# The scores of batch 1 moved into the transform of batch 0, and x of batch 2 transposed on TensorE

## The chip, the cores and the metric

The kernel runs on one core of a Trainium2 chip, in one launch. The metric is the device time of one execution in microseconds (us); less is better. Everything is written by hand for five engines: PE (TensorE, matrix products and transposes), ACT (ScalarE), DVE (VectorE), POOL (GpSimd) and SP, which issues most of the transfers.

## The reference

Two blocks follow each other. The first is an attention between 512 rows of `x` and 32 rows of `state` for each of 8 batches and 8 heads; the second mixes the 544 rows that come out with a two-dimensional Fourier transform, of which the real part is kept, then normalises each row and runs a two-layer network over it.

```python
def _attn_ref(x, state):                       # x (8, 8, 512, 64), state (8, 8, 32, 64)
    scores = scale * np.matmul(x, state.transpose(0, 1, 3, 2))
    a = softmax over the last axis of scores
    xread = np.matmul(a, state)
    scores2 = scale * np.matmul(state, x.transpose(0, 1, 3, 2))
    a2 = softmax over the last axis of scores2
    sread = np.matmul(a2, x)
    return np.concatenate([xread, sread], axis=2)

def _moe_ref(x, w_ch1, w_ch2):                 # x (8, 544, 512), w (512, 2048) and (2048, 512)
    mixed = np.real(np.fft.fft(np.fft.fft(x, axis=1), axis=2))
    u = x + mixed
    un = (u - mean) / np.sqrt(var + 1e-06)     # over the last axis
    return u + np.maximum(un @ w_ch1, 0.0) @ w_ch2
```

## The kernel before

The work goes batch by batch, and each batch passes five stages.

- **Load and cast.** `load_x(b)` brings x of a batch into the buffer `xs` (two of them, in turn), and `cast_x(b)` writes it as bf16 into `xin` (`xin0` for even batches, `xin1` for odd ones). From batch 1 on, the cast is one instruction on POOL (L117).
- **Attention, first half** (`attend`, its list `first`). The products need x and state with the other axis on the partitions: `turn_state` transposes state on PE into the PSUM tile `sTp`, and a copy (L311) makes `sT` of it. `turn_x(g)`, for g = 0 and 1, makes `xT` of x. For batches 0 and 1 it transposes on PE into the PSUM tile `xTp` (L322), with a copy by DVE for g = 0 and by ACT for g = 1 (L323). For batches from `by_dma` = 2 on, it is four transposing transfers, which SP issues (L316). `scores_t(g)` then forms `eTp` (L331) and its exponential `ET` on ACT (L333); `scores(i)` forms `esp` (L342) and `E` (L347).
- **Attention, second half** (`second`). `xread` and `sread` multiply `ET` and `E` with state and x (PSUM tiles `xrp`, `xfp`, `xlp`, `srp`), DVE divides by the sums, and `fold` adds and subtracts halves of the result on DVE to make `XE`, `XO` and `XN`.
- **Transform** (`transform`). `over_s(j)` is the transform over the rows (`gp`, L455 and L459; its copy `G`, L461 and L463), `over_d(k)` the one over the columns (`yp`, L473). `add(k, r)` makes a tile of `U` on DVE, `centre(k, r)` takes its statistics on DVE and subtracts the mean (`ub`, L490 on ACT), and `turn_u(k, r)` transposes `ub` into `unT`: on PE (`tp`, L501) with a copy by ACT (L502) for batches 0 and 1, by a transposing transfer later.
- **Network.** `layer1(b)` multiplies `unT` with the first weights (`ph`, L587 for batch 0 in quarter steps of 16 products of 128 columns, L577 for the others), and ACT writes `hT` (L589, L579). `layer2(b)` multiplies `hT` with the second weights (`po`, L643), DVE forms the output tile `ot` (L608), and SP stores it.

Both weights (`w` in the profile's rows) come through POOL's queue: the first from L254, the second from L269, which stands behind a small POOL instruction that reads the landed x of batch 2 (L267).

The order is written out by hand. Each engine executes its instructions in the order in which the program names them, and `weave` merges lists of steps: each list is spread evenly over a stretch from 0 to 1, and the steps are named in the order of these places. Every list here is so merged with the layer-1 or layer-2 products of an earlier batch. Three PSUM banks serve `sTp`, `xTp`, `eTp`, `esp`, `srp`, `gp`, `yp` and `tp` in turn (`qt`), three others serve `ph` and `po`, one pair serves `xread`. `warm(n)` puts n products without use on PE; `warmed` puts them behind each step of a list.

The program's middle names first the start of the transform of batch 0, then layer 1 of batch 0 with the rest of that transform (`t0[7:]`), with both halves of batch 1 (`s1` and `reads_next`), with the transform of batch 1 and with the first half of batch 2 (`scores_next`). `cast_x(2)` and the transfers that transpose x of batch 2 (`turned[2]`) stand at one tenth of it:

```python
for step in warmed(t0[:7], 2):
    step()
load_x(3)
scores_next, reads_after = attend(2)
weave((layer1(0), 0, 1), (t0[7:], 0.02, 0.3), (s1, 0.02, 0.32), (reads_next, 0.33, 0.57),
      (transform(1), 0.61, 1.0), ([lambda: (cast_x(2), turned[2]())], 0.1, 0.1), (scores_next, 0.5, 0.95),
      ([lambda: state_ones(2, B)], 0.5, 0.5), ([lambda: load_x(4)], 0.8, 0.8))
```

Of the kernel before, what the change touches and what calls it, by code (L numbers as in the profile page):

```python
# [28 lines left out]
def kernel(  # L29
# [8 lines left out]
    nc = tc.nc  # L38
# [72 lines left out]
    def cast_x(b):  # L111
        xs, t = xs_of[b], xin_bufs[b % 2]
        if b == 0:
            for si in (0, 1, 3, 2):
                nc.scalar.copy(t[:, si, 1:513], xs[:, si, :])
        else:
            nc.gpsimd.tensor_copy(t[:, :, 1:513], xs)  # L117
# [153 lines left out]
    def qt(name, dt=F32):  # L271
        return psQ.tile([128, 512 if dt == F32 else 1024], dt, name=name, tag="q")
# [12 lines left out]
        return mv, rstd  # L285


    by_dma = 2


    turned = {}

    def attend(b):
# [6 lines left out]
        sT = wk.tile([128, 4, 128], BF16, name="sT", tag="sT")  # L300
# [5 lines left out]
        def turn_state():  # L306
            p = qt("sTp", BF16)
            for pr in range(4):
                g, hp = pr // 2, pr % 2
                nc.tensor.transpose(p[:, pr * 128:(pr + 1) * 128], sb[:, g, 4 + 128 * hp:132 + 128 * hp], ident)  # L310
            nc.vector.tensor_copy(sT, p[:, 0:512].rearrange("p (a b) -> p a b", b=128))  # L311

        def turn_x(g):
            if b >= by_dma:
                for si in ((0, 1), (3, 2))[g]:
                    nc.sync.dma_start_transpose(out=xT[:, :, 128 * si:128 * si + 128], in_=xin[:, si, 1:513])  # L316
                return
            p = qt("xTp", BF16)
            for si in (0, 1, 3, 2):
                for k in range(2):  # L320
                    o = k * 512 + si * 128
                    nc.tensor.transpose(p[:, o:o + 128], xin[:, si, 1 + 128 * (2 * g + k):129 + 128 * (2 * g + k)], ident)  # L322
            (nc.vector.tensor_copy if g == 0 else nc.scalar.copy)(  # L323
                xT[:, 2 * g:2 * g + 2, :], p.rearrange("p (a b) -> p a b", b=S))


# [77 lines left out]
        def fold():  # L404
# [5 lines left out]
            nc.vector.tensor_sub(XO[:, 0:2, 1:256], Sm[:, :, 1:256], Sm[:, :, 511:256:-1])  # L410
            nc.vector.tensor_copy(XN[:, 0:2, 0:1], Sm[:, :, 256:257])

        first = ([] if b >= by_dma else [turn_state, lambda: turn_x(0), lambda: turn_x(1)]) + [
            lambda: scores_t(0),
            lambda: scores_t(1),
            lambda: scores(0),
            lambda: scores(1),
        ]
        if b >= by_dma:
            turned[b] = lambda: (turn_x(0), turn_x(1))  # L420
            first.insert(0, turn_state)
        second = [
# [15 lines left out]
    def transform(b):  # L438
        g4, bq = b // 4, b % 4
        XF, XR = XFs[b % 2], XRs[b % 2]  # L440
        XE, XO, XN = XEs[b % 2], XOs[b % 2], XNs[b % 2]
        G = wk.tile([128, 4, NM], BF16, name="G", tag="G")
        cos = [CT[:, 0, :], CT[:, 1, :], CL[:, bq, :]]
        sin = [ST[:, 0, :], ST[:, 1, :], SL[:, bq, :]]
        unT = wk.tile([128, DC, 512], BF16, name="unT", tag="unT", bufs=2)
        un_of[b] = unT
        U, ub, rstds = {}, {}, {}
        order = [(0, 1), (1, 1), (0, 0), (1, 0)] if b == B - 1 else [(0, 1), (0, 0), (1, 1), (1, 0)]

        def over_s(j):  # L450
            p = qt("gp")
            X, tab = (XE, cos) if j < 2 else (XO, sin)
            jj = j % 2
            for c in range(3):
                nc.tensor.matmul(p[:, 0:NM], lhsT=X[:, c, 128 * jj:128 * jj + 128], rhs=tab[c],  # L455
                                 start=(c == 0), stop=(c == 2 and j != 2))
            if j == 2:
                for c in range(3):
                    nc.tensor.matmul(p[:, 0:NM], lhsT=XN[:, c, :], rhs=cos[c], start=False, stop=(c == 2))  # L459
            if b == 0 and j < 2:  # L460
                nc.vector.tensor_copy(G[:, j, :], p[:, 0:NM])  # L461
            else:
                nc.scalar.copy(G[:, j, :], p[:, 0:NM])  # L463
            if j == 3:
                nc.gpsimd.tensor_copy(GLs[g4][:, :, 32 * bq:32 * bq + 32], G[:, :, 256:NM])  # L465

        yp_of = {}

        def over_d(k):
            U[k] = wk.tile([128, 2, 514], F32, name="U", tag="U", bufs=5)  # L470
            yp = yp_of[k] = qt("yp")
            for c in range(4):
                nc.tensor.matmul(yp, lhsT=G[:, c, 128 * k:128 * k + 128], rhs=T2[:, c, :],  # L473
                                 start=(c == 0), stop=(c == 3))

        def add(k, r):
            yp = yp_of[k]
            if r:
                nc.vector.tensor_add(U[k][:, 1, 1:512], yp[:, 1:512], XR[:, k, 1:512])  # L479
                nc.vector.tensor_add(U[k][:, 1, 512:513], yp[:, 0:1], XR[:, k, 512:513])  # L480
            else:
                nc.vector.tensor_add(U[k][:, 0, 0:512], yp, XF[:, k, 0:512])

        def centre(k, r):
            u = U[k][:, r, r:r + 512]
            mv, rstds[k, r] = stats_of(u, "rstd")
            t = ub[k, r] = wk.tile([128, 512], BF16, name="ub", tag="ub", bufs=5)
            ud = u if r == 0 else U[k][:, 1, 512:0:-1]
            if b in flipped:
                nc.scalar.activation(t, ud, AF.Identity, bias=mv[:, 0:1], scale=-1.0)  # L490
            else:
                nc.vector.tensor_scalar(t, in0=ud, scalar1=mv[:, 0:1], scalar2=None, op0=ALU.subtract)

        def turn_u(k, r):
            col = order.index((k, r)) * 128
            if b >= by_dma:
                nc.sync.dma_start_transpose(out=unT[:, :, col:col + 128], in_=ub[k, r])
                return
            tp = qt("tp", BF16)
            for j in range(DC):  # L500
                nc.tensor.transpose(tp[:, 128 * j:128 * j + 128], ub[k, r][:, 128 * j:128 * j + 128], ident)  # L501
            nc.scalar.copy(unT[:, :, col:col + 128], tp[:, 0:512].rearrange("p (a b) -> p a b", b=128))  # L502

        def done():
            tiles = []
            for k, r in order:
                if True:
                    u = U[k][:, r, 0:512] if r == 0 else U[k][:, r, 512:0:-1]
                    f0 = 128 * k + 1
                    dst = out[b, f0:f0 + 128, :] if r == 0 else (b, k)  # L510
                    tiles.append((u, rstds[k, r], dst))
            tiles_of[b] = tiles

        if b == 0:
            return [lambda j=j: over_s(j) for j in range(4)] + [
                lambda: over_d(0),
                lambda: (add(0, 1), centre(0, 1), over_d(1)),
                lambda: (add(0, 0), centre(0, 0), turn_u(0, 1)),
                lambda: (turn_u(0, 0), add(1, 1)),
                lambda: (centre(1, 1), add(1, 0)),  # L520
                lambda: (centre(1, 0), turn_u(1, 1)),
                lambda: (turn_u(1, 0), done())]
        return [
            lambda: over_s(0),
            lambda: over_s(1),
            lambda: over_s(2),
            lambda: over_s(3),
            lambda: (over_d(0), add(0, 1), add(0, 0)),
            lambda: centre(0, 1),
            lambda: (centre(0, 0), over_d(1), add(1, 1), add(1, 0)),  # L530
            lambda: (turn_u(0, 1), centre(1, 1)),
            lambda: (turn_u(0, 0), centre(1, 0)),
            lambda: turn_u(1, 1),
            lambda: (turn_u(1, 0), done()),
        ]
# [129 lines left out]
    def warmed(steps, n):  # L665
        return [lambda s=s: (s(), warm(n)) for s in steps if s is not None]
# [3 lines left out]
    s1, reads_next = attend(1)  # L670
    t0 = transform(0)
    weave((warmed(s0[:4], 8) + s0[4:], 0, 1), ([lambda: state_blocks(1, 2, nc.vector.tensor_copy)], 0.6, 0.6))
    weave((warmed(r0, 4), 0, 1), ([sines], 0.01, 0.01), ([more_sines], 0.3, 0.3), ([lambda: warm(56)], 1, 1))
    more_loads()
    for step in warmed(t0[:7], 2):
        step()
    load_x(3)
    scores_next, reads_after = attend(2)
    weave((layer1(0), 0, 1), (t0[7:], 0.02, 0.3), (s1, 0.02, 0.32), (reads_next, 0.33, 0.57),
          (transform(1), 0.61, 1.0), ([lambda: (cast_x(2), turned[2]())], 0.1, 0.1), (scores_next, 0.5, 0.95),  # L680
          ([lambda: state_ones(2, B)], 0.5, 0.5), ([lambda: load_x(4)], 0.8, 0.8))
    for b in range(1, B + 1):
        reads_next = reads_after
# [6 lines left out]
        if b + 2 < B:  # L690
            scores_next, reads_after = attend(b + 2)
# [38 lines left out]
```

## Time and profile before

| | us |
|---|---|
| median of 3 runs | 341.37 (341.16 to 342.92) |
| the profiled execution | 342.2 |
| span of the profiled execution, first to last instruction | 339.8 |
| PE busy | 316.3 |
| DVE busy | 167.1 |
| ACT busy | 144.8 |
| POOL busy | 62.3 |
| first product of layer 2 of batch 0 begins at | 72.04 |

The span is the part that the profile sees; 2.4 us of the profiled execution lie outside it. PE is the engine with the most work. From 72.04 us on layer 2 runs beside everything else, and the part before it is where the work of the first batches is brought up. A busy time of PE includes the end of the last product of a group, so a group that is followed at once by another shows a longer time than the distance between the two starts.

### The profile page before, as it was taken

To read this page: it belongs to the slowest core of one execution; us is meant where nothing else is said; L and a number is where in the kernel's file an instruction comes from. 1 tells how busy PE (TensorE), PEld (TensorE's weight loads), DVE (VectorE), ACT (ScalarE), POOL (GpSimd) and SP (SyncE) were. 2 spreads that over 40 slices of the span, in tenths; PEclk is the share of its full clock that TensorE was granted. 3 is DMA by queue.
4 is the path that set the end of the run, shared out by engine and by line. 5 is a ranking of instruction groups with operands and counts; after the bars stand their busy time and mean duration, and the time that the engine had idled before them with its cause. 6 is when DMAs were issued, how large, how long until landed. Compare 5 with 4: busy or idle time off the path is not lost.

```text
span 339.8 us, 5637 instructions
## 1 busy us (share of the span) xinstructions
PE 316.3 (93%) x2159; PEld 182.6 (54%) x2190; DVE 167.1 (49%) x421; ACT 144.8 (43%) x277; POOL 62.3 (18%) x144
## 2 busy tenths in 40 slices
PE   6896955979999999999999999999999999999995
PEld 5675844754555454455655455555545544455444
DVE  8775380546285447565183546555564555300122
ACT  7883842574434443343444443344344332234300
POOL 2189710230023002130023002400120012000000
PEclk9997995999999999999999999999999999999999
DMA  7999999017425661526624441632051207222055
GB/s 144 167 147 218 191 196 178 7 38 159 82 62 111 140 123 49 107 62 121 146 46 111 77 108 42 122 85 64 25 116 47 62 18 116 69 64 62 31 115 134
DMA packets 109258, 33.67 MB, mean 99 GB/s; under 512 B 100656, under 2 KB 105008, under 8 KB 109232
## 3 DMA queue, kind: packets, MB, share of 16 engines
q1 hardware_dynamic: 98512, 27.55, 39.9%
q0 software_dynamic: 4224, 4.19, 7.8%
q10 hardware_dynamic: 6496, 1.57, 2.3%
q8 instruction: 17, 0.28, 0.4%
q14 instruction: 9, 0.07, 0.1%
HBM read 22.04 MB, written 13.63 MB: 105 GB/s over the span
## 4 chain that ended last, share of the span: by engine, by line
PE 79%; DMA 6%; DVE 5%; POOL 3%; SPq 3%; ACT 1%; issue 1%; DVEq 0%; POOLq 0%; ACTq 0%
PE po L643 33%; PE ph L577 30%; PE yp L473 3%; DMA xs<-in_x_dram 3%; PE gp L455 3%; DMA xT<-xin 2%; PE eTp L331 2%; PE srp L378 2%; SPq L108 1%; SPq L316 1%; POOL xin L117 1%; PE xrp L359 1%; PE gp L459 1%; PE xfp L359 1%; POOL w L269 1%
## 5 line engine op out<-in xcount | busy, mean ns | idle before, releaser
L643 PE MATMUL po<-w,hT 128*128 128x512 bf16 x479 | 123.1, 379 | 0.9
L579 ACT ACTIVATE hT<-ph 128x512 bf16<-128x512 f32 x112 | 66.8, 597 | 111.2 <-PE ph L577 106.0
L577 PE MATMUL ph<-unT,w 128*128 128x512 bf16 x437 | 113.7, 379 | 0.4
L577 PEld LDWEIGHTS <-w 128*128 128x128 bf16 x576 | 51.1, 98 | 50.0
L643 PEld LDWEIGHTS <-hT 128*128 128x128 bf16 x496 | 48.0, 98 | 45.6
L608 DVE SCALAR_TENSOR_TENSOR ot<-po,rstd,U 128x512 f32<-128x512 f32 (+1 forms) x33 | 24.2, 733 | 47.7 <-PE po L643 45.3
L479 DVE TENSOR_TENSOR U<-yp,XR 128x511 f32<-128x511 f32 x16 | 10.9, 683 | 37.7 <-PE yp L473 35.9
L465 POOL COPY GL<-G 128x128 bf16<-128x128 bf16 x8 | 2.4, 298 | 146.0 <-ACT G L463 146.0
L279 DVE BATCH_NORM_STATS2 st<-U 128x6 f32<-128x512 f32 x32 | 21.8, 681 | 0.1
L284 POOL TENSOR_TENSOR rstd<-rstd,mhalf 128x1 f32<-128x1 f32 x34 | 20.1, 591 | 2.7
L587 PE MATMUL ph<-unT,w 128*128 128x128 bf16 x256 | 18.7, 231 | 1.5 <-ACT unT L502 1.5
L587 PEld LDWEIGHTS <-w 128*128 128x128 bf16 x256 | 17.1, 105 | 2.3 <-issue 1.6
L283 POOL TENSOR_TENSOR rstd<-mv,epst 128x1 f32<-128x1 f32 x34 | 6.5, 190 | 63.8 <-DVE mv L281 63.8
L463 ACT CAST G<-gp 128x288 bf16<-128x288 f32 x30 | 11.9, 397 | 14.7 <-PE gp L455 10.6
L663 PE MATMUL warm<-ident 128*128 128x128 bf16 x174 | 14.2, 234 | 3.7 <-POOL ident masks.py:199 3.3
L473 PE MATMUL yp<-T,G 128*128 128x512 bf16 x62 | 16.3, 379 | 0.1
L663 PEld LDWEIGHTS <-ident 128*128 128x128 bf16 x174 | 12.4, 106 | 5.1 <-POOL ident masks.py:199 3.3
L389 ACT ACTIVATE XR<-srp,rcs 32x64 bf16<-32x64 f32 x32 | 9.9, 308 | 12.1 <-DVE rcs L380 11.8
L333 ACT ACTIVATE ET<-eTp 128x512 bf16<-128x512 f32 x16 | 9.6, 599 | 10.4 <-PE eTp L331 10.4
L331 PE MATMUL eTp<-xT,sT 128*128 128x288 bf16 (+1 forms) x64 | 10.0, 281 | 4.0 <-DMA xT<-xin 3.8
L589 ACT ACTIVATE hT<-ph 128x512 bf16<-128x512 f32 x16 | 9.7, 610 | 9.5 <-PE ph L587 9.5
L117 POOL CAST xin<-xs 128x2048 bf16<-128x2048 f32 x7 | 13.2, 1888 | 0.0
(136 smaller groups left out, 337.9 us busy)
## 6 DMA issues: line engine op xcount, KB each, us to landing
xs<-in_x_dram SPq DMA_DIRECT2D x30, 256.0 KB, 4.8
w<-in_moe_w_ch_dram POOLq DMA_DIRECT2D x8, 512.0 KB, 10.1
out_dram<-ot SPq DMA_DIRECT2D x15, 256.0 KB, 3.0
r_dram<-ot SPq DMA_DIRECT2D x14, 256.0 KB, 2.0
out_dram<-r_dram SPq DMA_DIRECT2D x14, 256.0 KB, 3.6
xs<-in_x_dram ACTq DMA_DIRECT2D x2, 256.0 KB
l_dram<-ot SPq DMA_DIRECT2D x2, 256.0 KB, 2.2
r_dram<-ot ACTq DMA_DIRECT2D x2, 256.0 KB
```

Source lines behind the costliest of these rows:

```text
L117: nc.gpsimd.tensor_copy(t[:, :, 1:513], xs)
L279: nc.vector.bn_stats(st6, u)
L284: nc.gpsimd.tensor_tensor(rstd, rstd, mhalf, op=ALU.pow)
L331: nc.tensor.matmul(p[:, lo:hi], lhsT=sT[:, 2 * g + hp, :], rhs=xT[:, 2 * g + hp, src], start=(hp == 0), stop=(hp == 1))
L463: nc.scalar.copy(G[:, j, :], p[:, 0:NM])
L473: nc.tensor.matmul(yp, lhsT=G[:, c, 128 * k:128 * k + 128], rhs=T2[:, c, :], start=(c == 0), stop=(c == 3))
L577: nc.tensor.matmul(ph[:, o:o + n], lhsT=w1[:, c, f * 128:(f + 1) * 128], rhs=un_of[key][:, c, :], start=(c == 0), stop=(c == DC - 1))
L579: nc.scalar.activation(hT[:, per * i:per * i + per, :].rearrange("p a b -> p (a b)"), ph, AF.Relu, scale=-1.0 if key in flipped else 1.0)
L587: nc.tensor.matmul(ph[:, o:o + 128], lhsT=w1[:, c, f * 128:(f + 1) * 128], rhs=un_of[key][:, c, 128 * r:128 * r + 128], start=(c == 0), st ...
L608: nc.vector.scalar_tensor_tensor(ot[:, cols], in0=po_of[i][:, 0:cols.stop - cols.start], scalar=rstd, in1=u[:, cols], op0=ALU.mult, op1=AL ...
L643: nc.tensor.matmul(po_of[i], lhsT=h_of[key][:, f, i * 128:(i + 1) * 128], rhs=w2[:, f, :], start=(f == 0), stop=(f == FC - 1))
L663: nc.tensor.matmul(t[:, 0:128], lhsT=ident, rhs=ident, start=(i == 0), stop=(i == n - 1))
```

## The change

There are four edits, all in the part ahead of layer 2 of batch 0.

1. The first half of batch 1 begins earlier: `turn_x(0)` and `turn_state` stand behind `over_d(0)` of batch 0, and `turn_x(1)` stands two steps later, ahead of the first `turn_u`. The scores of batch 1 (`s1[3:]`) follow at the start of layer 1.
2. For batch 1 the copies change engines: g = 0 of `xT` and `sT` go to ACT, g = 1 of `xT` goes to DVE.
3. x of batch 2 is transposed on PE, with `turn_x(0)` and `turn_x(1)` inside `scores_next`, and no transfer does it any more. The bound of `turn_u` stays at 2.
4. The transform of batch 0 is cut into more steps, one thing each, and four more of them run ahead of layer 1, with `turn_u(0, 0)` the last of these. The stretches in `weave` are moved accordingly.

```diff
-    by_dma = 2
+    x_by_dma, u_by_dma = 3, 2
@@ turn_state
-            nc.vector.tensor_copy(sT, p[:, 0:512].rearrange("p (a b) -> p a b", b=128))
+            (nc.scalar.copy if b == 1 else nc.vector.tensor_copy)(sT, p[:, 0:512].rearrange("p (a b) -> p a b", b=128))
@@ turn_x
-            if b >= by_dma:
+            if b >= x_by_dma:
...
-            (nc.vector.tensor_copy if g == 0 else nc.scalar.copy)(
+            (nc.vector.tensor_copy if g == (b == 1) else nc.scalar.copy)(
@@ transform, batch 0
                 lambda: over_d(0),
-                lambda: (add(0, 1), centre(0, 1), over_d(1)),
-                lambda: (add(0, 0), centre(0, 0), turn_u(0, 1)),
-                lambda: (turn_u(0, 0), add(1, 1)),
-                lambda: (centre(1, 1), add(1, 0)),
-                lambda: (centre(1, 0), turn_u(1, 1)),
+                lambda: (add(0, 1), centre(0, 1)),
+                lambda: (add(0, 0), centre(0, 0)),
+                lambda: turn_u(0, 1),
+                lambda: over_d(1),
+                lambda: turn_u(0, 0),
+                lambda: (add(1, 1), centre(1, 1)),
+                lambda: (add(1, 0), centre(1, 0)),
+                lambda: turn_u(1, 1),
                 lambda: (turn_u(1, 0), done())]
@@ the middle
-    for step in warmed(t0[:7], 2):
+    for step in warmed(t0[:4], 2) + [t0[4], s1[1], s1[0], t0[5], t0[6], s1[2]] + warmed(t0[7:9], 2) + [t0[9]]:
         step()
...
-    weave((layer1(0), 0, 1), (t0[7:], 0.02, 0.3), (s1, 0.02, 0.32), (reads_next, 0.33, 0.57),
-          (transform(1), 0.61, 1.0), ([lambda: (cast_x(2), turned[2]())], 0.1, 0.1), (scores_next, 0.5, 0.95),
+    weave((layer1(0), 0, 1), (t0[10:], 0.02, 0.25), (s1[3:], 0.0, 0.16), (reads_next, 0.2, 0.55),
+          (transform(1), 0.58, 1.0), ([lambda: cast_x(2)], 0.1, 0.1), (scores_next, 0.55, 0.97),
```

The diff adds three lines ahead of layer 1, so its rows are three lines further down in the changed kernel (L587 becomes L590, L589 becomes L592).

What the order of ACT becomes, from the copies of the transform over the rows (`G`) on. Before:

```order
L463 CAST G<-gp 128x288 x2
L490 ACTIVATE ub<-U,mv 128x512 x2
L502 COPY unT<-tp 128x4x128
L589 ACTIVATE hT<-ph 128x4x128
L502 COPY unT<-tp 128x4x128
L589 ACTIVATE hT<-ph 128x4x128
L490 ACTIVATE ub<-U,mv 128x512
L323 COPY xT<-xTp 128x1024
```

And with the change:

```order
L463 CAST G<-gp 128x288 x2
L323 COPY xT<-xTp 128x1024
L311 COPY sT<-sTp 128x512
L490 ACTIVATE ub<-U,mv 128x512 x2
L502 COPY unT<-tp 128x4x128 x2
L333 ACTIVATE ET<-eTp 128x512
L592 ACTIVATE hT<-ph 128x4x128
```

The copies of batch 1's x and state now stand ahead of both `ub` of batch 0, and both copies into `unT` stand ahead of the first `hT`.

The order of SP, from the load of x of batch 2 on (`xin_98` is `xin0`, `xin_99` is `xin1`). Before:

```order
L108 DMA xs<-in_x_dram 128x8x64 x4
L108 DMA xs<-in_x_dram 1x8x64
L108 DMA xs<-in_x_dram 128x8x64 x4
L108 DMA xs<-in_x_dram 1x8x64
L316 DMA_TRANSPOSE xT<-xin_98 128x4x128 x4
L108 DMA xs<-in_x_dram 128x8x64 x4
L108 DMA xs<-in_x_dram 1x8x64
L316 DMA_TRANSPOSE xT<-xin_99 128x4x128 x4
```

And with the change:

```order
L108 DMA xs<-in_x_dram 128x8x64 x4
L108 DMA xs<-in_x_dram 1x8x64
L108 DMA xs<-in_x_dram 128x8x64 x4
L108 DMA xs<-in_x_dram 1x8x64
L108 DMA xs<-in_x_dram 128x8x64 x4
L108 DMA xs<-in_x_dram 1x8x64
L316 DMA_TRANSPOSE xT<-xin_99 128x4x128 x4
```

The loads of batches 2 and 3 stay where they were; the transposes of batch 2 are gone from between the loads of batches 3 and 4.

More of the change, by code (lines that the diff above doesn't have):

```diff
@@ L411, in fold @@
             nc.vector.tensor_copy(XN[:, 0:2, 0:1], Sm[:, :, 256:257])
-        first = ([] if b >= by_dma else [turn_state, lambda: turn_x(0), lambda: turn_x(1)]) + [
+        first = ([] if b >= x_by_dma else [turn_state, lambda: turn_x(0), lambda: turn_x(1)]) + [
             lambda: scores_t(0),
@@ L418, in attend @@
         ]
-        if b >= by_dma:
+        if b >= x_by_dma:
             turned[b] = lambda: (turn_x(0), turn_x(1))
@@ L495, in turn_u @@
             col = order.index((k, r)) * 128
-            if b >= by_dma:
+            if b >= u_by_dma:
                 nc.sync.dma_start_transpose(out=unT[:, :, col:col + 128], in_=ub[k, r])
```

## The prediction

> **What bounds the kernel now.** I read the busy times first, then the clock by slices, then the chain of waits.
>
> ```profile
> span 339.8 us, 5637 instructions
> PE 316.3 (93%) x2159; PEld 182.6 (54%) x2190; DVE 167.1 (49%) x421; ACT 144.8 (43%) x277; POOL 62.3 (18%) x144
> PE   6896955979999999999999999999999999999995
> PEclk9997995999999999999999999999999999999999
> PE 79%; DMA 6%; DVE 5%; POOL 3%; SPq 3%; ACT 1%; issue 1%; DVEq 0%; POOLq 0%; ACTq 0%
> ```
>
> PE is the bound. From the ninth slice on (a slice is 8.5 us) it is full at full clock; what can be won without taking products away lies ahead of that. Two dips of the clock, in the fourth and the sixth and seventh slice, stand beside two dips of PE. So I asked for the stretch from the first product over the columns of batch 0 to the first product of layer 2, and for who made PE wait in it.
>
> ```profile
> 24.05:72.04 47.99, 34.84 (x419) 28.48 (x419) 21.42 (x62) 25.14 (x50) 22.25 (x45) 0.86 0.91 146
> 72.04 1.03 PE L643 MATMUL po<-w,hT 128*128 128x512 bf16 x3
> PE eTp L331 <- DMA xT<-xin: 3.8, 1, 3.8
> PE tp L501 <- ACT ub L490: 3.2, 3, 1.5
> PE ph L587 <- ACT unT L502: 1.5, 1, 1.5
> PE gp L455 <- DVE XE L406: 1.4, 1, 1.4
> PE xfp L359 <- DVE XL L368: 1.0, 1, 1.0
> PE xrp L359 <- DVE XF L368: 0.9, 1, 0.9
> ```
>
> In 47.99 us PE is busy for 34.84 at a mean clock of 0.86: 13.15 us idle. The longest wait is for the transposing transfer of batch 2's x. Windows on the grid on which the clock changed (3.41 us) show the rest; behind the length stand the busy times of PE, its weight loads, DVE, ACT and POOL, and the third figure from the end is the clock.
>
> ```profile
> 26.66:30.07 3.41, 0.96 (x15) 0.84 (x16) 1.61 (x4) 1.92 (x3) 3.20 (x8) 1.00 1.22 203
> 30.07:33.48 3.41, 3.32 (x34) 3.16 (x32) 1.49 (x4) 1.18 (x2) 3.21 (x4) 0.50 1.17 232
> 43.72:47.13 3.41, 2.15 (x32) 1.67 (x30) 2.49 (x12) 2.25 (x6) 0.52 (x1) 1.00 1.23 198
> 47.13:50.55 3.42, 1.58 (x24) 1.21 (x21) 2.96 (x9) 1.19 (x2) 0.00 (x0) 1.00 1.23 198
> 50.55:53.96 3.41, 0.90 (x3) 0.28 (x3) 0.84 (x3) 0.40 (x1) 0.00 (x0) 0.50 1.39 110
> 53.96:57.37 3.41, 1.63 (x12) 1.49 (x13) 0.00 (x0) 0.58 (x1) 0.00 (x0) 0.50 1.32 218
> 57.37:60.79 3.42, 3.42 (x24) 2.63 (x22) 0.00 (x0) 1.15 (x4) 0.00 (x0) 0.50 0.91 147
> 67.61:71.03 3.42, 2.21 (x37) 1.86 (x34) 1.69 (x5) 3.22 (x7) 2.10 (x5) 1.00 0.00 0
> ```
>
> A window follows at half clock when PE was busy for 0.96, 1.58, 0.90 or 1.63 us of the one before, and at full clock after 2.15 or 2.21 (the next window after 43.72 and after 67.61 is granted 1.00). So between 1.6 and 2.15 us of work in a window lies a threshold, and idle time of PE is paid twice. The Trainium skill ("TensorE: Matmul & The Clock Gate", Part 1) has the same free-running window of about 3.4 us, but drops the clock after an idle window; here a window that is 46% busy was enough, so the trace decides.
>
> **The change part by part.** Prices first.
>
> ```profile
> 31.55 0.42 DVE L311 COPY sT<-sTp 128x512 bf16<-128x512 bf16 x1 [3.21 <-PE sTp L310]
> 31.98 0.58 ACT L502 COPY unT<-tp 128x512 bf16<-128x512 bf16 x1 [0.20 <-PE tp L501]
> 33.08 0.69 DVE L323 COPY xT<-xTp 128x1024 bf16<-128x1024 bf16 x1 [0.44 <-PE xTp L322]
> 33.99 0.49 PEld L322 LDWEIGHTS <-xin 128*128 128x128 bf16 x8
> 34.05 0.61 PE L322 MATMUL xTp<-ident,xin 128*128 128x128 bf16 x8
> 35.35 1.00 ACT L323 COPY xT<-xTp 128x1024 bf16<-128x1024 bf16 x1
> 38.70 1.06 PE L587 MATMUL ph<-unT,w 128*128 128x128 bf16 x16
> 39.59 0.40 PE L342 MATMUL esp<-sT,xT 128*128 128x64 bf16 x8
> 25.12 0.69 DVE L479 TENSOR_TENSOR U<-yp,XR 128x511 f32<-128x511 f32 x1 [1.84 <-PE warm L663]
> 26.85 0.72 ACT L490 ACTIVATE ub<-U,mv 128x512 bf16<-128x512 f32 x1 [2.31 <-DVE mv L281]
> 28.37 0.72 ACT L490 ACTIVATE ub<-U,mv 128x512 bf16<-128x512 f32 x1 [0.80 <-DVE mv L281]
> 29.62 1.47 PE L587 MATMUL ph<-unT,w 128*128 128x128 bf16 x16 [1.48 <-ACT unT L502]
> ```
>
> A group of 16 products shows 1.06 us, but the next begins 0.89 after it (38.70 to 39.59): about 0.056 per product of 128 columns, and 0.17 of tail when PE then waits. By that, eight transposes hold PE 0.45 to 0.49, four hold it 0.22, and a group `eTp` 0.43.
>
> *x of batch 2.* Removed: the wait of 3.8, and four transfers. Added on PE: 16 transposes, 2 × 0.49 = +1.0. I cost the copies (0.69 on DVE, 1.00 on ACT) at nothing: each lies beside a `ph` group of 0.89 or six `gp` products; uncovered they cost 1.7. The Trainium skill ("TensorE: Matmul & The Clock Gate", Part 4) gives about 275 ns per transpose in one kernel; by it 16 cost 4.4 instead of 1.0, and the sum below would be 3.4 smaller. Eight in 0.61 us speak against that here.
>
> *The clock at 50 to 61.* PE's products of three windows at 0.50, 0.90 + 1.63 + 3.42 = 5.95 us, would take half: −3.0. It needs the windows before to be fuller, which the next two parts give.
>
> *Batch 1 in the transform of batch 0.* `over_d(0)` ends at 25.1, where DVE's addition begins. PE now goes on at once with eight transposes and four of state (to 25.8), ACT copies from 25.8 to 26.8 and, at unT's price of 0.58, to 27.4. The second eight wait for that first copy (same PSUM bank): 26.9 to 27.3. `ub` of the first tile slips from 26.85 to 27.4; that of the second cannot come before its statistics, 28.37 as before, so `unT` is as early as before. Between them PE does `tp`, `over_d(1)`, the second `tp` and `eTp`. I get the first `ph` at 30.1, 0.5 later than 29.62, with 0.45 × 2 + 0.22 + 0.22 + 0.43 = 1.8 of work done ahead that came after it: −1.3 (between 0, if the copies on ACT hold `ub` back by more than another 1.3, and −2.9, both idle pieces of 1.5 in the rows above).
>
> *The clock at 30.* The window before it then has some 2.4 us of PE work instead of 0.96, above 2.15: half of 3.32, −1.7.
>
> *The other waits.* 13.15 idle less 3.8 less 2.9 leaves 6.4. I walked the new order through, PE by the spacings above, ACT and DVE by the durations in the rows, each step from the one it waits for: fourth `ph` ends 34.8, `sread` waits 0.3 for its copy, the reads of batch 1 (one PSUM pair, DVE between) wait 0.3, 0.3 and 1.4 up to 42.7, the fold 0.7 at 45.5, the first transposes of batch 2 at 46.4, `yp` of batch 1 at 50.1, its four `tp` wait 0.6 and 0.8, and layer 2 begins at 59.3. These waits are 4.5, less eight tails of 0.17 is 3.1 idle: −3.3 (between 0 and −6.4). I put it down to batch 1's `E` and batch 0's `ub` being asked for earlier than they are read.
>
> *Queues and steps that move.*
>
> ```profile
> 40.78 1.89 POOL L117 CAST xin<-xs 128x2048 bf16<-128x2048 f32 x1
> 42.70 7.80 SPq L316 DMA_TRANSPOSE xT<-xin  x4
> 50.55 7.17 SPq L108 DMA_DIRECT2D xs<-in_x_dram  x5
> L254 POOL DMA_DIRECT2D w<-in_moe_w_ch_dram x4: 766/775/942, 16.9 to 19.3; - x4
> DMA to landing us min/median/max: 5.6/8.8/12.6
> L269 POOL DMA_DIRECT2D w<-in_moe_w_ch_dram x4: 760/775/787, 35.9 to 38.2; - x4
> DMA to landing us min/median/max: 7.6/11.5/16.1
> ```
>
> On POOL the cast of batch 2 moves behind one more pair of `rstd` instructions, to end about 43.5 instead of 42.7; PE needs it at 46.4. On SP the load of batch 4 follows that cast, so it begins at 43.5 instead of 50.55, beside the second weights. Those landed by 38.2 + 16.1 = 54.3 at the latest, with four transposing transfers beside them; now the load takes that place. Layer 2 asks for the first quarter at 59.3 and for the last 5 us later. The first weights are asked for sooner too (the last quarter at 33.9 in the walk), and had landed by 19.3 + 12.6 = 31.9. Both 0; a late landing would cost its lateness. Warm-up products: 14 become 12, −0.1, left out.
>
> Sum: −3.8 + 1.0 − 3.0 − 1.3 − 1.7 − 3.3 = −12.1 (the walk alone, 72.04 to 59.3, says −12.7). Behind 72 PE is full and its work is unchanged, so the whole of it should reach the end. The profiled execution, 342.2 with 2.4 outside its span, would become 330.1; the median of the runs shown, 341.37, is 0.8 lower, and I put the changed kernel's median at **329.4 us**.
>
> **The rivals.**
> *The clock falls once or twice more.* In the walk the emptiest windows hold 1.7 us (25.0 to 28.4) and 2.0 (39.3 to 42.7), inside the unknown band of 1.6 to 2.15, and where the grid falls is not the program's choice. Price: half of some 3.3 us of work, 1.7 a window: 331.1, or 332.8 for two. By the Trainium skill ("TensorE: Matmul & The Clock Gate", Part 4) transposes do not count as activity for the clock; then the window ahead of 30 holds only about 1 us and the term of −1.7 is lost, which is this case. Against it: the window 67.61:71.03 stayed at full clock after with 2.21, of which two transpose groups of 0.4 are part.
> *ACT becomes the bound of the stretch.* It gets 1.0 + 0.6 more ahead of `ub`, and 1.0 for batch 2. If that eats the gains of the reordering, there remain the transfer's wait and its clock: −3.8 − 3.0 + 1.0 = −5.8, 335.6. For it: 3.22 of 3.42 us busy in 67.61:71.03. Against: ACT is busy for 25.14 of 47.99 over the whole stretch, and DVE loses as much as ACT gains.
> *Slower: a POOL wait in the place of the transfer's.* PE takes its instructions in order, so a late cast of batch 2 stops `ph` too. It has 46.4 − 43.5 = 2.9 us to spare; each further us costs one, and the clock. Slower than before only if the cast ended beyond about 59, with the gains of 12 used up; at 63 it would be 346. The row of the cast shows no wait ahead of it, and one pair of `rstd` is the 0.8 already counted.
> *Better:* all of the 6.4 goes: 326.3.
>
> **How the numbers follow.** Forecast (gain 11 to 14) 0.58; clock 0.20; ACT 0.13; better 0.07; slower 0.02. 0.5% (1.7 us) is about what a measurement tells from no change. All but the last case lie beyond it: faster 0.97, the same 0.01, slower 0.02. The range runs from 327.0 (the walk and half of what the other waits leave) to 333.0 (two more windows at half clock) and leaves out the ACT case.
>
> **What would show it.** Right: no wait of PE for `xT<-xin` of batch 2; `xTp` three times; first `ph` near 30.1; clock 1.00 from 26 to 72; first `po` at 58.5 to 60.5; the distance from there to the end unchanged (267.8). Wrong: 0.50 in a window between 28 and 46 (the clock); PE waiting for ACT's `ub`, `unT` or `xT` for more than 5 us (ACT); a wait of `xTp` for POOL; a wait of `po` for the second weights, which would mean that the load of batch 4 holds them back.

## The result, and the profile after

| | us | ratio to before, 95% interval |
|---|---|---|
| before, in the same series | 341.26 (340.9 to 342.92, 4 runs) | |
| after | 331.31 (328.6 to 331.63, 4 runs) | 0.9681 [0.9634, 0.9727] |
| after, in a second series (below) | 328.91 (328.58 to 329.59, 4 runs) | 0.9616 [0.9592, 0.9639] |

The kernel is faster by 10 to 13 us; the forecast was 329.4. The eight runs of after fall into two groups: three at 331.2 to 331.6 and five at 328.6 to 329.6. The profiled execution of the first series is one of the upper group (331.23). Its page begins:

```profile
span 329.3 us, 5692 instructions
PE 315.1 (96%) x2204; PEld 182.2 (55%) x2204; DVE 169.0 (51%) x421; ACT 146.3 (44%) x279; POOL 62.8 (19%) x144
PE   6988969899999999999999999999999999999995
PEclk9999979999999999999999999999999999999999
PE 84%; DVE 5%; DMA 4%; POOL 3%; SPq 2%; ACT 1%; issue 1%; DVEq 0%; POOLq 0%; ACTq 0%
```

Behind the start, PE and the clock now dip together in one slice only, the sixth. DMA has fallen from 6% to 4% of the chain, DVE has stayed at 5%. The waits of PE between 24 and 62 us, and the stretch to the first `po` with the two windows of the clock's grid in it that stand out (columns as in the prediction):

```profile
PE xrp L359 <- DVE XF L368: 2.9, 1, 2.9
PE xTp L322 <- ACT xT L323: 0.9, 1, 0.9
PE tp L501 <- ACT E L347: 0.7, 1, 0.7
PE tp L501 <- ACT ub L490: 0.5, 1, 0.5
PE tp L501 <- DVE U L482: 0.3, 1, 0.3
PE srp L378 <- ACT unT L502: 0.2, 1, 0.2
```
```profile
24.06:61.79 37.73, 31.96 (x435) 27.72 (x432) 23.52 (x62) 25.53 (x50) 21.61 (x45) 0.95 0.96 169
40.98:44.39 3.41, 0.45 (x3) 0.17 (x4) 3.23 (x8) 0.58 (x1) 2.67 (x4) 1.00 1.22 197
44.39:47.80 3.41, 3.41 (x31) 3.28 (x32) 2.97 (x13) 0.60 (x1) 0.00 (x0) 0.50 1.22 195
```

The stretch is 10.3 us shorter (37.73 for 47.99). The wait for the transposing transfer is gone, and those for `ub`, `unT`, `XL` and `XE` are gone or small. What is left in one piece is 2.9 us for an eviction of DVE, and the window with it, in which PE did 0.45 us, is followed by one at half clock. The timeline at that place shows why DVE was late, and the view of its line that it was late only once in eight calls:

```profile
30.06 1.06 PE L590 MATMUL ph<-unT,w 128*128 128x128 bf16 x16
41.01 1.90 POOL L117 CAST xin<-xs 128x2048 bf16<-128x2048 f32 x1
41.09 1.96 DVE L399 TENSOR_TENSOR XE<-XL 32x256 bf16<-32x256 bf16 x1
43.59 0.69 DVE L368 TENSOR_TENSOR XF<-xfp,rs 128x512 bf16<-128x512 f32 x1
44.34 0.60 PE L359 MATMUL xrp<-stb,ET 128*128 128x260 bf16 x2 [2.90 <-DVE XF L368]
61.79 1.03 PE L646 MATMUL po<-w,hT 128*128 128x512 bf16 x4
...
L399 DVE TENSOR_TENSOR XE<-XL x8: 274/284/1955, 21.2 to 252.8; 32x256 bf16<-32x256 bf16 x8
```

L399 is the addition that folds the low rows of batch 1, `XL[0:256] + XL[512:256:-1]`, with both inputs in SBUF. It takes 0.28 us as a rule and took 1.96 here: it began 0.08 us behind POOL's cast of batch 2 and ended 0.14 behind that cast's end.

### The profile page after: what moved, and what is told of

Read it like the earlier page. It is cut to its first block, busy times and chain, and to the rows that moved or that the text cites. A ratio compares the mean times of both kernels' runs of the same rounds, so it can differ in the third digit from the quotient of the medians.

```text
span 329.3 us, 5692 instructions
## 1 busy us (share of the span) xinstructions
PE 315.1 (96%) x2204; PEld 182.2 (55%) x2204; DVE 169.0 (51%) x421; ACT 146.3 (44%) x279; POOL 62.8 (19%) x144
## 4 chain that ended last, share of the span: by engine, by line
PE 84%; DVE 5%; DMA 4%; POOL 3%; SPq 2%; ACT 1%; issue 1%; DVEq 0%; POOLq 0%; ACTq 0%
PE po L646 35%; PE ph L580 32%; PE yp L473 3%; DMA xs<-in_x_dram 3%; PE gp L455 3%; PE ph L590 2%; PE eTp L331 2%; PE srp L378 2%; SPq L108 1%; PE xrp L359 1%; POOL w L269 1%; DMA out_dram<-ot 1%; PE xfp L359 1%; PE gp L459 1%; PE esp L342 1%
## 5 line engine op out<-in xcount | busy, mean ns | idle before, releaser
L646 PE MATMUL po<-w,hT 128*128 128x512 bf16 x496 | 125.2, 379 | 0.0
L580 PE MATMUL ph<-unT,w 128*128 128x512 bf16 x448 | 115.0, 379 | 0.0
L283 POOL TENSOR_TENSOR rstd<-mv,epst 128x1 f32<-128x1 f32 x34 | 7.2, 211 | 63.6 <-DVE mv L281 63.5
L590 PE MATMUL ph<-unT,w 128*128 128x128 bf16 x256 | 18.0, 228 | 0.0
L590 PEld LDWEIGHTS <-w 128*128 128x128 bf16 x256 | 16.6, 103 | 0.5
L389 ACT ACTIVATE XR<-srp,rcs 32x64 bf16<-32x64 f32 x32 | 9.9, 309 | 10.3 <-DVE rcs L380 10.0
L359 PEld LDWEIGHTS <-ET 128*128 128x128 bf16 x80 | 7.3, 98 | 11.7 <-DVE XF L368 3.7
L592 ACT ACTIVATE hT<-ph 128x512 bf16<-128x512 f32 x16 | 9.4, 604 | 8.0 <-PE ph L590 8.0
L492 DVE TENSOR_SCALAR ub<-U,mv 128x512 bf16<-128x512 f32 x24 | 12.3, 512 | 0.9
```

The lines of the kernel that those rows point to most:

```text
L359: nc.tensor.matmul(ph[:, 0:260], lhsT=ET[:, g, c0:c0 + 128], rhs=rhs, start=True, stop=True)
L580: nc.tensor.matmul(ph[:, o:o + n], lhsT=w1[:, c, f * 128:(f + 1) * 128], rhs=un_of[key][:, c, :], start=(c == 0), stop=(c == DC - 1))
L590: nc.tensor.matmul(ph[:, o:o + 128], lhsT=w1[:, c, f * 128:(f + 1) * 128], rhs=un_of[key][:, c, 128 * r:128 * r + 128], start=(c == 0), st ...
L646: nc.tensor.matmul(po_of[i], lhsT=h_of[key][:, f, i * 128:(i + 1) * 128], rhs=w2[:, f, :], start=(f == 0), stop=(f == FC - 1))
```

## The experiments

My theory after the first result: DVE's addition cannot run beside POOL's cast, and that costs 1.7 us and then the window at half clock. The rivals: the addition is slow for a reason of its own; the clock fell for another reason; or the time is set by the copies that changed engines. The first two runs take the change apart.

**x of batch 2 on PE, alone.** The kernel before, with edit 3 only:

```diff
-    by_dma = 2
+    x_by_dma, u_by_dma = 3, 2
...
-          ... ([lambda: (cast_x(2), turned[2]())], 0.1, 0.1), (scores_next, 0.5, 0.95),
+          ... ([lambda: cast_x(2)], 0.1, 0.1), (scores_next, 0.5, 0.95),
```

> The kernel before with one part of the change alone: x of batch 2 is transposed on PE, everything else stays in its old order. If the terms of the prediction are separate, it gains the wait for the transfer (3.8) and the half clock of 50 to 61 (3.0), less 1.0 for the transposes: 5.8 us, about 335.5. The rival, that the parts only work together (because without the reordering the next wait stands behind the transfer's, and the clock stays low), gives less than 3 us, above 338.

Measured: 333.58 (333.53 to 335.05; before 342.35 in this series), ratio 0.9755 [0.9719, 0.979]: 8.8 us of gain, 3.0 more than expected. Its first `po`, and three windows of its grid:

```profile
64.08 1.03 PE L643 MATMUL po<-w,hT 128*128 128x512 bf16 x4
```
```profile
24.28:27.69 3.41, 2.30 (x16) 1.15 (x14) 2.10 (x5) 1.09 (x3) 3.38 (x9) 1.00 1.24 206
27.69:31.10 3.41, 1.58 (x26) 1.46 (x27) 0.99 (x3) 1.49 (x3) 3.19 (x8) 1.00 1.24 228
31.10:34.52 3.42, 3.13 (x57) 3.01 (x55) 3.10 (x7) 2.18 (x4) 2.67 (x4) 1.00 1.10 204
```

The idle pieces of 1.5 us around 28 are there as in the kernel before, yet no window falls to half clock: the grid, laid here from the fall of the clock behind the last product (331.48), stands 2.4 us earlier and cuts them in two, 2.30 and 1.58 us of work instead of 0.96 in one window. So the window at half clock at 30 is a matter of where the grid falls. One of the four runs, the one of 335.05 us, has a mean clock of 0.995 instead of 1.000, which is what one window at half clock makes; no trace shows where it stood. The first `po` comes 7.96 us earlier; the prediction's terms for the transfer (−3.8 + 1.0) and for both places of half clock (−3.0, −1.7) make −7.5.

**The new order, alone.** The kernel after, with x of batch 2 turned by transfers again:

```diff
-    x_by_dma, u_by_dma = 3, 2
+    x_by_dma, u_by_dma = 2, 2
...
-          (transform(1), 0.58, 1.0), ([lambda: cast_x(2)], 0.1, 0.1), (scores_next, ...
+          (transform(1), 0.58, 1.0), ([lambda: (cast_x(2), turned[2]())], 0.1, 0.1), (scores_next, ...
```

> The changed kernel, but x of batch 2 by the transposing transfers again. By the prediction the reordering keeps 1.3 + 1.7 + 3.3 = 6.3 us if its gains are its own: about 335. The rival: PE only arrives earlier at the same transfer, which lands near 55.7 us whatever PE does, so that all but about 1 us of the 6.3 is given back there, 340, with a wait of PE for xT of 8 us or more and at least three windows at half clock.

Measured: 337.12 (336.83 to 338.07), ratio 0.9845 [0.9809, 0.9881]: 5.2 us of gain, between the two theories. The longest wait, and the timeline around the transfers:

```profile
PE eTp L331 <- DMA xT<-xin: 6.7, 1, 6.7
```
```profile
41.49 0.28 DVE L399 TENSOR_TENSOR XE<-XL 32x256 bf16<-32x256 bf16 x1
42.96 1.89 POOL L117 CAST xin<-xs 128x2048 bf16<-128x2048 f32 x1
44.88 6.12 SPq L316 DMA_TRANSPOSE xT<-xin  x4
55.27 1.04 PE L331 MATMUL eTp<-xT,sT 128*128 128x288 bf16 x4 [6.67 <-DMA xT<-xin]
68.00 1.03 PE L646 MATMUL po<-w,hT 128*128 128x512 bf16 x4
```

Most of what the order gains ahead of the transfer is given back at it: PE comes to it 3.3 us earlier (48.60 for 51.93) and waits 2.9 longer, and three windows (51.0 to 61.3) are at half clock. What stays lies behind it: from that product to the first `po` it is 12.73 us instead of 16.30. Which of the moved steps saves how much there, no run shows. The two parts alone gain 8.8 and 5.2, 14.0 together; the whole change gained 13.1 in the second series. They nearly add up. And here the addition came ahead of the cast, took 0.28, and PE waited 1.2 at `xrp`, not 2.9.

**The cast early.** The kernel after, with the cast of batch 2 as soon as its x has landed, ahead of the issues of the second weights on POOL:

```diff
         nc.gpsimd.tensor_copy(gate, xs_of[2][:, :, 0])
+        cast_x(2)
         for q in range(4):
             nc.gpsimd.dma_start(out=w2[...], in_=w2v[...])
...
-          (transform(1), 0.58, 1.0), ([lambda: cast_x(2)], 0.1, 0.1), (scores_next, ...
+          (transform(1), 0.58, 1.0), (scores_next, ...
```

> The changed kernel with POOL's cast of batch 2 ahead of the loads of the second weights, at about 35 to 37 us, where VectorE works on PSUM. Theory: the addition of XL that took 1.96 us (0.28 in its other seven calls) was held until POOL's cast, which reads and writes SBUF, had ended. Then here it takes 0.28, TensorE's wait for XF falls from 2.9 to 1.4, the window at half clock goes, the first product of layer 2 begins at 59.0 to 60.0 instead of 61.8, and the time is 328 to 329.5. The rival, that the addition was slow for another reason (the load of batch 4 or the semaphore of POOL's clears) and the clock falls anyway in this emptier stretch: the addition stays above 1 us or the half-clock window stays, 331 to 332.

```profile
35.68 1.89 POOL L117 CAST xin<-xs 128x2048 bf16<-128x2048 f32 x1
41.08 0.30 DVE L400 TENSOR_TENSOR XE<-XL 32x256 bf16<-32x256 bf16 x1
42.67 0.40 PE L360 MATMUL xrp<-stb,ET 128*128 128x260 bf16 x2 [1.24 <-DVE XF L369]
59.19 1.03 PE L647 MATMUL po<-w,hT 128*128 128x512 bf16 x4
```

Measured: 328.70 (328.66 to 329.13), ratio 0.9605 [0.9575, 0.9634], clock 1.00 throughout. The addition takes 0.30, `xrp` waits 1.24, and the first `po` begins at 59.19; the prediction's walk had 1.4 and 59.3.

**The cast in four pieces**, at its old place:

```diff
-            nc.gpsimd.tensor_copy(t[:, :, 1:513], xs)
+            if b == 2:
+                for si in range(4):
+                    nc.gpsimd.tensor_copy(t[:, si, 1:513], xs[:, si, :])
+            else:
+                nc.gpsimd.tensor_copy(t[:, :, 1:513], xs)
```

> The changed kernel with POOL's cast of batch 2 cut into four instructions of a quarter each, at the same place. If VectorE is shut out for as long as one POOL instruction lasts, the addition of XL waits for one quarter at most and takes 0.3 to 0.8 us, TensorE's wait is 1.4 to 2.0, and the time 328.5 to 330. If the two engines share bandwidth, or POOL keeps its turn from one instruction to the next, the addition still takes about 1.9 us and the time stays at 331.

Measured: 328.99 (328.71 to 329.14), ratio 0.9609 [0.958, 0.9639]. In its profile the four casts begin at 42.79, behind the addition at 41.09, so the two did not meet, and that made me look at what sets the cast's start. But the casts met the fold that follows:

```profile
42.79 2.76 POOL L119 CAST xin<-xs 128x512 bf16<-128x512 f32 x4
44.39 0.70 DVE L409 TENSOR_TENSOR Sm<-XF,XR 128x1028 bf16<-128x1028 bf16 x1
45.12 0.71 DVE L410 TENSOR_TENSOR XE<-Sm 128x512 bf16<-128x512 bf16 x1
...
L119 POOL CAST xin<-xs x4: 613/616/1096, 42.8 to 44.5; 128x512 bf16<-128x512 f32 x4
```

`Sm`, an addition with both inputs in SBUF, starts at 44.39, at the end of the third cast and just ahead of the fourth (44.5), and takes 0.70 us, no more than alone; that cast takes 1.10 instead of 0.61, to 45.55. The next addition, `XE`, comes at 45.12 beside it and takes 0.71 instead of 0.43, to 0.28 behind the cast's end. So the hold goes both ways, for the one that comes second, and lasts one instruction: DVE came in between two casts, so POOL does not keep its turn, and `Sm` at its full speed speaks against a shared bandwidth.

**The idle window filled.** The kernel after, with 40 products without use ahead of the last read of batch 1:

```diff
-            lambda: (xread(384, True, "xrp", XR[:, 1, 1:513]), fold()),
+            lambda: (warm(40) if b == 1 else None, xread(384, True, "xrp", XR[:, 1, 1:513]), fold()),
```

> The kernel after, with 40 warm-up products put on PE into the wait of 2.9 us ahead of the last read of batch 1 (some 40 x 0.056 = 2.2 us of work without use). The cast and the addition stay where they collide. Theory (a window follows at half clock because the one before it is nearly empty): the addition L399 still takes 1.9 to 2.0 us and `xrp` still comes at about 44.3, but the window 41 to 44.4 now holds some 2.7 us of PE work, so none of the next is at half clock: 1.2 to 1.7 us less, first `po` at 60.1 to 60.6, time 329.6 to 330.2. Rival (the clock falls for another reason than PE's idle time): a window at half clock stays, 331.2 to 331.5.

Measured: 329.44 (329.16 to 330.29), ratio 0.9654 [0.9623, 0.9686], no window at half clock. The number is close to the one expected (329.6 to 330.2), and the experiment failed all the same: the cast began at 42.95, the addition at 41.19 took 0.28, and there was no window of 0.45 to fill. The separate proof that the fill would have saved the clock wasn't had.

**The copies back.** The kernel after without edit 2:

```diff
-            (nc.scalar.copy if b == 1 else nc.vector.tensor_copy)(sT, ...)
+            nc.vector.tensor_copy(sT, ...)
...
-            (nc.vector.tensor_copy if g == (b == 1) else nc.scalar.copy)(
+            (nc.vector.tensor_copy if g == 0 else nc.scalar.copy)(
```

> The kernel after, with the copies of batch 1's state and first x half put back on DVE and the second half on ACT (edit 2 of the change undone for them). Theory (the exchange of the copies shortens DVE's way to the statistics of batch 0): first `ph` later by up to the two copies, 0.42 + 0.69 = 1.1 us, at 30.6 to 31.2, and the time 331.8 to 332.5. Rival (only the order matters, since ACT has 0.3 us more to copy in the new form): first `ph` at 29.9 to 30.2, time 331.0 to 331.5, or less if the reads then miss the cast.

```profile
27.13 0.68 DVE L479 TENSOR_TENSOR U<-yp,XR 128x511 f32<-128x511 f32 x1
29.63 0.61 PE L501 MATMUL tp<-ident,ub 128*128 128x128 bf16 x4 [2.09 <-ACT ub L490]
```
```profile
25.44:28.86 3.42, 1.50 (x21) 1.16 (x20) 2.60 (x7) 0.01 (x1) 3.31 (x12) 1.00 1.25 207
28.86:32.27 3.41, 2.64 (x13) 1.54 (x14) 1.49 (x4) 2.61 (x4) 3.20 (x7) 0.50 1.26 239
```

Measured: 331.88 (331.76 to 332.03), ratio 0.9722 [0.9692, 0.9752]. The time fits the first theory, the mechanism is larger than it said: the first `ph` comes at 32.96, 2.9 us later than in after, not 1.1. DVE's addition for the first tile begins at 27.13 for 25.13, since the two copies stand ahead of it and, before them, the wait for the transposes that they copy (the first begins at 26.19). PE waits 2.1 us for `ub`, and that window, with 1.50 us of work, is followed by one at half clock. The addition of the fold did not meet the cast here (42.10 to 43.99, the addition at 43.98), so the fair comparison is with 328.7 to 328.9: edit 2 is worth 3 us, of which some 1.3 is the window at half clock (half of its 2.64).

**The cast twice**, to double the suspected cost:

```diff
-            nc.gpsimd.tensor_copy(t[:, :, 1:513], xs)
+            for _ in range(2 if b == 2 else 1):
+                nc.gpsimd.tensor_copy(t[:, :, 1:513], xs)
```

> The kernel after, with POOL's cast of batch 2 done twice in a row at its place (the second writes the same values again). Theory (DVE's addition with two SBUF inputs cannot run while POOL's cast runs): the addition L399 takes 3.8 to 3.9 us instead of 1.96, or 1.96 if it slips in between the two casts and the next DVE instruction takes the rest; `xrp` waits 4.6 to 4.9 us instead of 2.9, first `po` at 63.5 to 65, time 333.0 to 335.0. Rival (the addition is slow for a reason of its own, and the cast has no part in it): 1.96 us and a wait of 2.9 as before, 331.2 to 331.6, since the first reader of the cast comes at 46.4 or later and the two casts end by 44.9.

```profile
41.49 0.28 DVE L400 TENSOR_TENSOR XE<-XL 32x256 bf16<-32x256 bf16 x1
41.91 3.85 POOL L118 CAST xin<-xs 128x2048 bf16<-128x2048 f32 x2
44.79 1.50 DVE L406 TENSOR_TENSOR Sm<-XF,XR 128x1028 bf16<-128x1028 bf16 x1
46.82 0.42 PE L456 MATMUL gp<-CT,XE 128*128 128x288 bf16 x2 [1.35 <-DVE XE L407]
60.41 0.81 PE L647 MATMUL po<-w,hT 128*128 128x512 bf16 x3
```

Measured: 330.31 (329.83 to 332.53, six runs: two at 332.4 and 332.5, four at 329.8 to 330.6), ratio 0.9697 [0.966, 0.9735]. Neither expectation held for the profiled run, because again the cast began behind the addition. But its second half met the next DVE addition with two SBUF inputs, `Sm`, which took 1.50 us instead of 0.69 and ended 0.5 behind the casts' end; PE waited 1.35 for it. Which addition is hit, and whether one is, depends on the moment; one that is hit waits for the cast. The two upper runs have a mean clock of 0.995, again what one window at half clock makes; no trace of them is kept.

**A POOL instruction that only writes.** In the kernel with the early cast, a memset over the x just cast (no longer needed) stands at the cast's old place; first once, then three times in a row.

```diff
-          (transform(1), 0.58, 1.0), (scores_next, ...
+          (transform(1), 0.58, 1.0), ([lambda: [nc.gpsimd.memset(xs_of[2], 0.0) for _ in range(3)]], 0.1, 0.1), (scores_next, ...
```

> The kernel with the early cast (POOL casts batch 2 ahead of the second weights), and at the old place of the cast a POOL memset of 128x2048 f32 over the x just cast, which is no longer needed: some 1.8 us in which POOL writes SBUF and reads none. Theory (the lock needs a POOL instruction that reads SBUF, as the Trainium skill has it in "SBUF — State Buffer"): the addition, now L400, stays at 0.28, `xrp` waits 1.2, time 328.6 to 329.0. Rival (any POOL instruction of that length that touches SBUF locks it): the addition takes 1.7 to 1.9, `xrp` waits 2.7 to 2.9, a window at half clock, time 331.0 to 331.5.

Once: 328.98 (328.74 to 329.16), ratio 0.9636 [0.9606, 0.9666]. The memset ran from 43.12 to 44.92, behind the low rows' addition (41.48), so it did not put the question.

> As the write-only kernel, with the memset three times in a row (5.4 us, from about 42.5 or 43.1 on), so that it spans the fold of batch 1: DVE's Sm addition at about 44.8 (L406, 0.70 to 0.72 alone; 1.50 beside the doubled cast), then XE and XO from Sm (0.43 and 0.42). Each reads two SBUF operands. Theory (only a POOL instruction that reads SBUF locks): Sm stays at 0.70 to 0.73 and XE and XO at 0.42 to 0.44 with memsets running beside them. Rival (a write locks as well): Sm takes over 1.0 us and ends with a memset. The time says little: the rstd of the next tile waits behind the memsets, up to 3.6 us; 328.7 to 332.

```profile
43.43 5.53 POOL L684 MEMSET xs<- 128x2048 f32 x3
44.79 0.69 DVE L406 TENSOR_TENSOR Sm<-XF,XR 128x1028 bf16<-128x1028 bf16 x1
46.20 0.92 DVE L412 COPY XN<-Sm 128x2 bf16<-128x2 bf16 x1
...
L412 DVE COPY XN<-Sm x8: 152/166/922, 22.6 to 256.4; 128x2 bf16<-128x2 bf16 x8
```

Three times: 329.32 (328.79 to 330.51), ratio 0.9631 [0.9598, 0.9665]. `Sm` runs its 0.69 us wholly beside memsets: a write does not hold up an addition with two SBUF inputs. What it does hold up is the small copy behind, 0.92 us instead of 0.17, up to about the end of the second memset (three take 5.53, so the second ends near 43.43 + 2 × 1.84 = 47.1). The same profile has the contrast: `Sm` of batch 0, at 20.39, took 0.92 beside a POOL copy that reads SBUF (L218, 20.27 to 20.74).

**The kernel after, once more**, to see whether the two groups come from where the cast stands.

> The kernel after, unchanged. In it POOL waits for the load of batch 2's x, issues the second weights (3.0 us) and does four short steps before the cast, so the cast begins 6.1 us after the load's landing; in the runs so far that was between 41.0 and 43.0, and DVE's addition L399 comes at 41.1 to 41.5. Theory (the lock, decided in each run by when the load lands): the times fall into two groups with nothing between, near 331.3 (cast first) and near 328.7 (addition first), with at least one run in each; in the profiled run, L399 takes over 1.4 us if the cast starts within 1.6 us ahead of it and some 0.28 if it starts behind it. Rival (the addition is slow in this kernel for a reason of its own, and the single 328.6 was a stray): all runs at 331.2 to 331.7, L399 at 1.96 wherever the cast stands.

```profile
span 326.7 us, 5661 instructions
41.09 0.28 DVE L399 TENSOR_TENSOR XE<-XL 32x256 bf16<-32x256 bf16 x1
41.49 1.89 POOL L117 CAST xin<-xs 128x2048 bf16<-128x2048 f32 x1
42.67 0.40 PE L359 MATMUL xrp<-stb,ET 128*128 128x260 bf16 x2 [1.23 <-DVE XF L368]
59.20 1.03 PE L646 MATMUL po<-w,hT 128*128 128x512 bf16 x3
```

Measured: 328.91 (328.58 to 329.59), ratio 0.9616 [0.9592, 0.9639]. All four runs are in the lower group, so the expectation that both would show in one series missed. The profile settles the cause: the same program, the addition at 41.09 in both profiles, the cast at 41.01 in one and at 41.49 in the other. The difference comes from the load of batch 2's x. POOL's small read of it, which waits for its landing, stands here:

```profile
35.40 0.19 POOL L267 COPY gate<-xs 128x4 f32<-128x4 f32 x1 [1.64 <-DMA xs<-in_x_dram]
```
and, in the profile of the first series, here:
```profile
34.92 0.19 POOL L267 COPY gate<-xs 128x4 f32<-128x4 f32 x1 [1.41 <-DMA xs<-in_x_dram]
```

From there to the cast it is 6.09 us in both, the issues of the weights and seven short steps. A load that lands 0.5 us earlier lets the cast in first, and costs 2.5 us (331.23 for 328.74). For the two profiled runs this is shown; that the six others divide by it too is inferred from their times and their mean clocks (0.995 and 0.994 in the two of the upper group, 0.998 to 1.000 in the four of the lower).

**Two remedies more.** The folds of the low rows moved behind the last read of batch 1, in the kernel after, and then with the early cast too:

```diff
-            if b:
+            if b > 1:
                 fold_low(True)
                 fold_low(False)
...
-            if b == 0:
+            if b <= 1:
                 fold_low(True)
                 fold_low(False)
```

> The kernel after, with the two folds of the low rows of batch 1 (L399, L401) moved from behind `xlp` into the fold after the last read; the cast is untouched. Theory (the addition must not stand beside the cast; the Sm addition can be hit instead, when the load lands late): with an early landing (cast 41.0 to 42.9) nothing of DVE with two SBUF inputs stands beside it, the wait at `xrp` falls to 0.5 to 0.7, the fold has 0.6 more: 328.5 to 329.2; with a late one (cast to 44.9) Sm is held up and `gp` waits up to 1.3: 329.2 to 330.2. No run at 331. Rival (the order of the additions does not matter): 331.2 to 331.7 in most runs.

> Both remedies: the early cast and the folds of the low rows moved behind the last read. If the wait of 1.2 at `xrp` that the early cast leaves is DVE's time for the two folds and one eviction, it falls to 0.6, and the fold behind it gets 0.6 longer: 328.4 to 328.9, the same as the early cast alone (328.7). Rival (one of the two waits is covered by other work): 0.5 less, 328.1 to 328.3.

Measured: 329.24 (329.12 to 329.36), ratio 0.9623 [0.9603, 0.9643], and 328.79 (328.7 to 328.97), ratio 0.961 [0.959, 0.9631]. No run is at 331 in either. The wait at `xrp` fell from 1.2 to 1.0 only, not to 0.6: DVE, free earlier, then waits 0.49 us for the product of the tile before, whose eviction PE waits for. So the second remedy adds nothing to the first. The early cast alone, 328.70, which both together do not beat, is about as good as after at its best, and without the group at 331 in its four runs.

## Why the prediction was right, and where it was not

**The walk** held where nothing collided. First `ph`: 30.1 said, 30.06 measured. Wait at `xrp`: 1.4 said, 1.23. First transposes of batch 2: 46.4 said, 46.35. First `po`: 59.3 said, 59.20 in the second series and 59.19 with the early cast. From there to the end nothing changed: 267.5 us after (329.3 − 61.79, and 326.7 − 59.20), 267.8 before. Two sums of the prediction are a tenth off: its seven waits make 4.4, not 4.5, and 341.37 − 12.1 is 329.3. Ahead of layer 1 stand ten steps of batch 0's transform instead of seven, three more and not four; the only work among them that stood behind before is `turn_u(0, 0)`, as the prediction's sum has it. The second profile shows every sign that the prediction named for being right. The first lacks two, the clock of 1.00 up to 72 and a first `po` by 60.5.

**The step that failed** is the one on POOL's cast, under "queues and steps that move". It gave the cast a price of 0 because its only reader comes later (46.4), and the term "the other waits" took every DVE duration from rows in which the cast stands elsewhere. In the kernel before, the addition came at 45.96, 3.3 us behind the cast's end; the new order asks for it at 41.09, and the cast starts at 41.0 to 43.0. The walk itself had the cast from about 41.6 to 43.5, so the question of who stands beside it could have been put. Its price, when the cast is first: the addition takes 1.96 − 0.28 = 1.7 us more, and `xrp` begins 1.67 later (44.34 for 42.67). From there to the first `gp` it is 3.87 us instead of 2.94: 3.41 us of work at half clock cost 1.7, less some 0.7 of idle time ahead of `gp` that only the undisturbed profile has (a wait of 0.53 and the tail of 0.17 before it). From `gp` to the first `po` the two are alike (13.58 and 13.59). That makes 2.6, which is 61.79 − 59.20. That 331.31 lies inside the range all the same is luck as far as the cause goes: the range was made for windows that the walk's own waits empty. The Trainium skill states the lock ("SBUF — State Buffer", "Who interferes with whom"): DVE with two SBUF inputs and a GpSimd instruction that reads SBUF exclude each other for a whole instruction. The trace agrees (0.28 to 1.96, 0.69 to 1.50), and I had not weighed it.

**The clock.** Its rival, one window more at 331.1, gives the upper group's time, but by a cause that it did not name: the window held 0.45 us of work, where the walk's emptiest hold 1.7 and 2.0. The bound can now be told closer. Windows with 1.50 us (the copies back) and 1.58 (before) were followed by half clock, another with 1.58 (x on PE alone) was not, nor any at full clock with 1.94 or more; near the bound, the busy time of the profile doesn't tell which. A window that is itself at half clock has another bound: 2.59 us (the new order alone, from 54.45) was followed by half clock, 2.64 (the copies back, from 28.86) by full, so the 0.90 and 1.63 in the prediction's list, from such windows, say nothing of the first. The term of −1.7 at 30 came, but not only by the step it was put down to: with the gap unfilled, another place of the grid avoided it too. One window at half clock takes 0.005 off a run's mean clock (1.7 of 340 us). By that measure most runs of before, at 0.985, have three such windows, and the profiled one, at 0.980, from which the prediction took its terms for the clock, has four.

**Transposes on PE**: `xTp` comes for three batches, in two groups of 0.61 us each, and PE does not wait for a copy of batch 2. The term of −3.8 + 1.0 fits, and so does that of −3.0.

**ACT as the bound**: refuted, its `ub`, `unT` and `xT` make PE wait 1.6 us in all. The exchange of the copies, which loads ACT more, is what lets the order work: without it 3 us are lost.

**A late cast, late weights**: not seen (the 0.3 us that `xTp` waits for POOL in the second profile, at 25.14, are for the cast of batch 1). No wait of PE for anything is listed behind 62 us, and the load of batch 4 beside the second weights cost nothing.

## What to carry to other kernels

When an order moves, ask for each instruction on DVE and POOL not only who reads its result but who stands beside it, as far as loads can shift it: here a cast with 3 us of slack cost 2.6 us. A margin of some 0.1 us between two engines that exclude each other makes a kernel whose time depends on when a load lands; take the pair apart in the program (here the cast went ahead of the issues it had no need to wait for). And an experiment on such a pair has to be read in its profile first: three of these (the cast in four, the fill, the single memset) did not contain the collision they were made for, and two (the cast in four, the cast twice) had another in its place.

## What was not expected of the hardware

A POOL memset left DVE's additions with two SBUF inputs alone (0.69 us, as without it), but held up a DVE copy of two columns from SBUF to SBUF, for 0.92 us instead of 0.17. The Trainium skill has both cases ("SBUF — State Buffer", "Who interferes with whom"): an addition with two SBUF inputs contends only with a GpSimd instruction that reads SBUF, a copy can run in a mode that contends with any. The rows agree with it; whether this copy ran in that mode, no run here shows by itself.
